# Linear attention and MLP on one core: first tiles in another order, key weights by halves, masks in parts, a query at tile 14, the last tile by halves

## The chip, the cores and the metric

The kernel runs on one core of one Trainium2 chip. The metric is the device time of one execution in microseconds. It was run three times before the change: 780.79, 780.26 and 780.09 us, median 780.26. One more execution was profiled.

## The reference

Four layers over a residual stream x of 2048 tokens by 576 channels in bfloat16: attention (A), MLP (B), A, B with the same weights. Cut to what matters:

```python
def _A_ref(x, wqkv, wo):                       # H = 32 heads of Dh = 18
    qkv = (x @ wqkv) ... q, k, v = qkv[0], qkv[1], qkv[2]
    phi = lambda t: jnp.where(t > 0, t + 1, jnp.exp(t)) + 1e-6
    pq, pk = phi(q), phi(k)
    kv = jnp.einsum("bhsd,bhse->bhde", pk, v)
    z = jnp.einsum("bhsd->bhd", pk)
    num = jnp.einsum("bhqd,bhde->bhqe", pq, kv)
    den = jnp.einsum("bhqd,bhd->bhq", pq, z)[..., None] + 1e-6
    return (num / den) ... @ wo
def _B_ref(x, w1, b1, w2, b2):                 # F = 4608
    y = _layernorm(x, axis=-1)
    h = _gelu(jnp.einsum("bsd,df->bsf", y, w1) + b1)
    return jnp.einsum("bsf,fd->bsd", h, w2) + b2

x = A_x
x = x + _A_ref(_layernorm(x, axis=-1), A_wqkv, A_wo)
x = x + _B_ref(_layernorm(x, axis=-1), B_w1, B_b1, B_w2, B_b2)
x = x + _A_ref(_layernorm(x, axis=-1), A_wqkv, A_wo)
x = x + _B_ref(_layernorm(x, axis=-1), B_w1, B_b1, B_w2, B_b2)
```

## The kernel before

**Tiles.** x stays in SBUF as 16 tiles of 128 tokens (`x_sb`). A normalized tile y is transposed into `yT`, five blocks of 128 channels by 2048 tokens, of which the last block is half zeros. All weights are loaded once and stay.

**Order.** Each engine executes its instructions in the order in which the program writes them down: the helper class at L44 ties every instruction of VectorE (DVE), ScalarE (ACT), GpSimd (POOL) and SyncE (SP) to the one before it, so that nearly all of them carry the line L52 in the profile, and `pe` (L159) does the same for TensorE, whose matmuls carry L166. Waits between engines are put in from what each instruction reads and writes. So a step that is written earlier runs earlier on every engine that it uses, and an engine that waits holds up all that is written behind.

**Loads.** `load_x(t)` brings a tile of x (one DMA of 144 KB), `load_wkv(a, b)` columns a to b of the key and value weights (two DMAs: 512 rows, and 64 rows). SP issues x 0, x 1, all key columns (0 to 576), x 2, the first 252 value columns, x 3, the other value columns, x 4 to 9, then the query weights (seven DMAs), x 10 to 15, and in the tile loop the weights for later, one piece a tile.

**Head.** `warm` issues matmuls on zeros (L236: 12 of them, and 4 more at L753 behind the first transposes). `Norm` (L256) makes one normalized tile in steps that the program places one by one: `half_stats` and `close_stats` (two `bn_stats`, one `bn_aggr` and a small sum for the variance plus epsilon, all on DVE), `rstd` (a power on POOL, and on ACT's tiles a second product there), `norm` (y on DVE or ACT), `transposed` (five transposes on TensorE and a copy by ACT or DVE, or a DVE transpose and DMAs).

**Attention, tile loop** (`layer_A`, L386). For a tile t: `k_proj` makes keys in two halves of 288 columns, each with five matmuls into a PSUM bank and one exp by ACT; its `finish` on DVE makes phi with one operation on both halves and one on each half. `v_proj` makes values in two groups of columns (252 and 324) in one pair of banks, `accB`, of which there is a single one; ACT copies 504 of the columns out and DVE the last 72. `kv_acc` adds pk times v over all tiles in the pair `accA`. In the first layer (`placed` false) keys are made one tile ahead and the norms run two to three tiles ahead in the same loop; in the third layer (`placed` true) the rows were normalized in the MLP before.

**Queries.** There are 20 query blocks (5 groups of heads by 4 chunks of 512 tokens), each of five matmuls of 512 columns, an exp and a relu on ACT and two sums on DVE. `q_next` takes the next of them. With `late`, the two sums are put off and done by `finish(n)`. Before, tiles 3 to 10 (first layer) or 4 to 11 (third) issue one each, one stands behind the loop, two behind the last `kv_acc`, and the others in the code that follows.

**Behind the loop.** The last `kv_acc` releases the mask product `kvT` on DVE (it reads `maskz`), and this the sums `z_ps`, the products with wo, the denominators (`den_stage`) and the output (`wo_stage`), interleaved with query blocks and with the norms of the first four MLP tiles.

**Masks.** `masks_a` and `masks_b` build six constant tiles on POOL by fills and `affine_select`. They are called behind tiles 12 and 13 of the first layer.

**Last tile.** In the MLP (`LayerB.run`) one tile's output is 36 x 2 matmuls that alternate between the two halves of 288 columns, then `residual` adds x and bias in one DVE operation, and in the last layer the tile goes out with one DMA.

Of the kernel before, what the change touches and what calls it, by code (L numbers as in the profile page):

```python
# [15 lines left out]
P = 128  # L16
# [4 lines left out]
G = 5  # L21
# [14 lines left out]
def build(tc, A_x, A_wqkv, A_wo, B_w1, B_b1, B_w2, B_b2, out, n_layers=4):  # L36
    nc = tc.nc
    with ExitStack() as ctx:
# [60 lines left out]
        def masks_a():  # L99
            sel, fill = pool.affine_select, pool.memset  # L100
            fill(maskz[:], 1.0)
            sel(out=maskz[:], in_=maskz[:], compare_op=ALU.is_ge, fill=0.0,
                base=0, pattern=[[-DH, 7], [0, DH]], channel_multiplier=1)
            sel(out=maskz[:], in_=maskz[:], compare_op=ALU.is_ge, fill=0.0,
                base=DH - 1, pattern=[[DH, 7], [0, DH]], channel_multiplier=-1)
            sel(out=maskz[:], in_=maskz[:], compare_op=ALU.not_equal, fill=1.0,
                base=-126, pattern=[[0, 7], [0, DH]], channel_multiplier=1)
            fill(z_row[:], 0.0)
            sel(out=z_row[:], in_=z_row[:], compare_op=ALU.not_equal, fill=1.0,
                base=-126, pattern=[[0, 1]], channel_multiplier=1)  # L110
            fill(head_sel[:], 1.0)
            sel(out=head_sel[:], in_=head_sel[:], compare_op=ALU.is_ge, fill=0.0,
                base=0, pattern=[[126, G], [-DH, H]], channel_multiplier=1)
            sel(out=head_sel[:], in_=head_sel[:], compare_op=ALU.is_ge, fill=0.0,
                base=DH - 1, pattern=[[-126, G], [DH, H]], channel_multiplier=-1)

            fill(zsel[:], 0.0)
            sel(out=zsel[:, 0, :], in_=zsel[:, 0, :], compare_op=ALU.not_equal, fill=1e-6,
                base=-126, pattern=[[0, H]], channel_multiplier=1)

        def masks_b():
            sel, fill = pool.affine_select, pool.memset
            fill(quad_mask[:], 1.0)
            sel(out=quad_mask[:], in_=quad_mask[:], compare_op=ALU.is_ge, fill=0.0,
                base=0, pattern=[[-32, 4], [0, P]], channel_multiplier=1)
            sel(out=quad_mask[:], in_=quad_mask[:], compare_op=ALU.is_ge, fill=0.0,
                base=31, pattern=[[32, 4], [0, P]], channel_multiplier=-1)
            fill(head_bc[:], 0.0)
            hb = head_bc[:, :, 0:126].rearrange("p g (h d) -> p g h d", h=7)
            for quad in range(4):  # L130
                sel(out=hb, in_=hb, compare_op=ALU.not_equal, fill=1.0,
                    base=-32 * quad, pattern=[[-7, G], [-1, 7], [0, DH]], channel_multiplier=1)
# [89 lines left out]
        load_wkv(0, D)  # L222
# [13 lines left out]
        warm(NWARM + 2)  # L236
# [19 lines left out]
        class Norm:  # L256
# [13 lines left out]
            def close_stats(self):  # L270
                stt = self.stt
                self.mv = work.tile([P, 2], F32, name="ln_mv", bufs=8)
                vec.bn_aggr(out=self.mv[:], in_=stt[:])
                self.u = work.tile([P, 1], F32, name="ln_u", bufs=8)
                if self.kind == "A":
                    vec.tensor_scalar(out=self.u[:], in0=self.mv[:, 1:2], scalar1=EPS, scalar2=None, op0=ALU.add)
                else:
                    vec.tensor_scalar(out=self.u[:], in0=self.mv[:, 1:2], scalar1=1.0 + EPS, scalar2=EPS * EPS,
                                            op0=ALU.mult, op1=ALU.add)

            def rstd(self):
# [104 lines left out]
        def layer_A(li, next_kind, before_tile, mid_tile, rows_ahead, after_tile, q_tiles, placed, mlp):  # L386
# [76 lines left out]
            if ahead:  # L463
                k_proj(0)
# [387 lines left out]
```

## Time and profile before

| What | Value |
|---|---|
| Median of three executions | 780.26 us |
| The profiled execution | 780.55 us |
| Its span, first to last instruction | 778.8 us |
| Granted TensorE clock, mean | 1.000 |
| TensorE matmul busy | 768.2 us (99%), 6563 instructions |
| VectorE busy | 285.5 us (37%) |
| ScalarE busy | 315.9 us (41%) |
| GpSimd busy | 96.3 us (12%), 174 instructions |
| DMA | 25.69 MB, in the first 58 us near all of the 16 engines' time |

In a timeline line the columns are: start in us from the beginning of the span, busy us, engine, line, operation, output and inputs by the program's names, shapes, and how many instructions were merged; in brackets the idle time of the engine before it and what ended that. PE is TensorE's matmul, PEld its weight load, SPq a DMA that SP issues. The end of a matmul is modelled, so the next may begin before the end that is shown.

### The profile page before, as it was taken

Reading aid. Unit: us, or ns where it says so; the run is one execution under the profiler, and the core shown is the slowest. Engines: PE = TensorE matmul, PEld = TensorE weight load, DVE = VectorE, ACT = ScalarE, POOL = GpSimd, SP = SyncE. Lnnn points to the kernel's source line nnn. Section 1 sums busy time; section 2 is a strip of 40 time slices with the busy share of each in tenths; the row PEclk is TensorE's granted clock in tenths of the full one; section 3 lists DMA queues with packets and bytes.
Section 4 is the critical chain, followed back from the end, with each engine's and each line's share of the span. In section 5 each row is a group of like instructions: output and inputs, shape, how many; then the busy total and the mean of one; then the engine's idle time right before and its main releaser. Section 6 shows DMA issues by size and latency. Waiting matters only on the chain.

```text
span 778.8 us, 15414 instructions
## 1 busy us (share of the span) xinstructions
PE 768.2 (99%) x6563; PEld 489.2 (63%) x6583; DVE 285.5 (37%) x700; ACT 315.9 (41%) x656; POOL 96.3 (12%) x174
## 2 busy tenths in 40 slices
PE   8999999999999999999999999999999999999998
PEld 5775555675477457646777754557745764675476
DVE  7885853436223412500354576534140230110000
ACT  4667744203720660174035577341066027305700
POOL 3114200212011101200200010002120120010010
PEclk9999999999999999999999999999999999999999
DMA  8990000010001101010000000000100100010000
GB/s 217 251 343 6 1 1 2 1 35 18 19 3 32 36 1 28 8 35 1 2 11 24 1 2 1 1 2 17 42 10 1 40 26 2 8 50 10 1 8 24
DMA packets 50334, 25.69 MB, mean 33 GB/s; under 512 B 35098, under 2 KB 50266, under 8 KB 50266
## 3 DMA queue, kind: packets, MB, share of 16 engines
q1 hardware_dynamic: 50266, 24.71, 11.6%
q8 instruction: 51, 0.84, 0.5%
q14 instruction: 17, 0.14, 0.1%
HBM read 15.79 MB, written 2.36 MB: 23 GB/s over the span
## 4 chain that ended last, share of the span: by engine, by line
PE 91%; ACT 4%; DVE 3%; issue 1%; POOL 0%; DVEq 0%; POOLq 0%
PE m_ps L166 36%; PE h_ps L166 19%; PE hp_ps L166 15%; PE v_ps L166 5%; PE k_ps L166 5%; PE q_ps L166 4%; ACT units L52 3%; PE wo_ps L166 3%; PE kvacc L166 1%; PE warm_ps L166 1%; DVE x_sb L52 1%; PE rden_ps L166 1%; DVE units L52 1%; PE tp L314 1%; DVE ln_st L52 1%
## 5 line engine op out<-in xcount | busy, mean ns | idle before, releaser
L166 PEld LDWEIGHTS <-units 128*128 128x128 bf16 (+2 forms) x2624 | 254.5, 98 | 75.8 <-issue 10.9
L166 PE MATMUL m_ps<-w_sb,units 128*128 128x288 bf16 x2304 | 283.6, 286 | 0.0
L166 PEld LDWEIGHTS <-w_sb 64*128 64x128 bf16 x2304 | 124.5, 94 | 138.1 <-issue 7.7
L166 PE MATMUL hp_ps<-yT,w_sb 64*128 64x512 bf16 x1152 | 175.7, 376 | 0.0
L166 PE MATMUL h_ps<-yT,w_sb 64*128 64x512 bf16 x1152 | 151.2, 376 | 1.0 <-DVE units L52 0.6
L52 ACT COPY relay_sb<-relay_sb 128x1 f32<-128x1 f32 x144 | 27.5, 191 | 289.4 <-PE h_ps L166 268.0
L52 DVE TENSOR_TENSOR x_sb<-m_ps,xo 128x576 bf16<-128x576 f32 x32 | 24.2, 757 | 323.4 <-PE m_ps L166 323.4
L52 ACT ACTIVATE units<-h_ps,b1T 128x512 bf16<-128x512 f32 x144 | 91.2, 684 | 44.5 <-PE h_ps L166 42.6
L52 ACT ACTIVATE units<-hp_ps,b1T 128x512 bf16<-128x512 f32 x144 | 96.2, 688 | 0.0
L52 POOL TENSOR_TENSOR xo<-x_sb,b_bc 128x576 f32<-128x576 bf16 x32 | 40.8, 1274 | 420.1 <-DVE x_sb L52 249.1
L166 PEld LDWEIGHTS <-yT 128*128 128x128 bf16 x640 | 61.0, 97 | 19.0 <-issue 1.9
L52 POOL TENSOR_TENSOR ln_rstd<-ln_u,neg_half 128x1 f32<-128x1 f32 x64 | 35.1, 549 | 209.2 <-DVE ln_u L52 209.2
L166 PE MATMUL h_ps<-yT,w_tail 64*128 64x512 bf16 x144 | 54.1, 376 | 0.0
L166 PE MATMUL hp_ps<-yT,w_tail 64*128 64x512 bf16 x144 | 54.1, 376 | 0.0
L52 DVE BATCH_NORM_STATS2 ln_st<-x_sb 128x6 f32<-128x288 bf16 x128 | 51.5, 442 | 2.3 <-DMA x_sb<-in_A_x_dram 1.9
L52 ACT ACTIVATE units<-q_ps 128x512 bf16<-128x512 f32 x80 | 43.4, 603 | 14.5 <-PE q_ps L166 9.9
L52 DVE STREAM_TRANSPOSE shared<-y_ring 128x640 bf16<-128x640 bf16 x40 | 33.3, 837 | 42.6 <-DMA yT<-shared 40.7
L166 PE MATMUL q_ps<-yT,wq_sb 128*128 128x512 bf16 x186 | 47.1, 379 | 1.2 <-ACT units L52 0.3
L166 PE MATMUL wo_ps<-shared,units 126*128 126x288 bf16 (+1 forms) x320 | 44.9, 286 | 1.0
L166 PE MATMUL v_ps<-wkv_sb,yT 128*128 128x252 bf16 (+1 forms) x320 | 44.4, 285 | 1.4 <-DVE v_ring L52 1.4
L166 PE MATMUL k_ps<-wkv_sb,yT 128*128 128x288 bf16 x320 | 44.3, 286 | 0.0
L52 DVE TENSOR_TENSOR x_sb<-wo_ps,x_sb 128x576 bf16<-128x576 f32 x32 | 24.2, 757 | 50.8 <-PE wo_ps L166 49.6
(69 smaller groups left out, 393.9 us busy)
## 6 DMA issues: line engine op xcount, KB each, us to landing
yT<-shared SPq DMA_DIRECT2D x160, 40.0 KB, 1.9
w_sb<-in_B_w_dram SPq DMA_DIRECT2D x12, 432.0 KB, 8.2
w_sb<-in_B_w_dram SPq DMA_DIRECT2D x9, 512.0 KB, 8.7
x_sb<-in_A_x_dram SPq DMA_DIRECT2D x16, 144.0 KB, 3.4
out_dram<-x_sb SPq DMA_DIRECT2D x16, 144.0 KB, 1.7
wkv_sb<-in_A_wqkv_dram SPq DMA_DIRECT2D x1, 576.0 KB
w_tail<-in_B_w_dram SPq DMA_DIRECT2D x2, 288.0 KB, 11.5
wo_sb<-in_A_wo_dram SPq DMA_DIRECT2D x1, 567.0 KB
```

Source lines behind the costliest of these rows:

```text
L52: inst = issue(*args, **kw)
L166: return pe(nc.tensor.matmul(out_, lhsT=lhsT, rhs=rhs, start=start, stop=stop, **kw))
L314: pe(nc.tensor.transpose(out=tp[:, k, :], in_=self.y[:, k * P:(k + 1) * P], identity=ident[:]))
```

## The change

1. **Key weights by halves.** The 576 key columns come with two calls of `load_wkv` instead of one, that is four DMAs instead of two.
2. **First tiles.** The warm-up is 9 matmuls, not 12. The zeroing of the query weights' padding on POOL (five fills) comes ahead of the first norm. Behind the first tile's transposes, `begin0` writes out the order: key halves, transposes of tiles 1 and 2, statistics of tiles 2 and 3, phi, and the values of tile 0 in two parts. In tile 0 of the loop phi of tile 1 stands around the norm of tile 3.
3. **Variance sum.** It goes from DVE (`close_stats`) to POOL (`rstd`), for all 64 norms.
4. **Masks in parts.** Nine batches, one behind each of the tiles 2 to 10 of the first layer; the first instruction of a batch waits for the DVE's copy of that tile's values.
5. **Query at tile 14.** Tile 14 of both attention layers issues a query; one of the two behind the last `kv_acc` is gone, and one `finish` less stands later.
6. **Values of tile 0 in the third layer.** ACT copies all 576 columns.
7. **Last tile by halves.** In the last layer tile 15 makes its 36 matmuls of the first half, adds and stores it, then the second half.

```diff
-        load_wkv(0, D)
+        load_wkv(0, HALF)
+        load_wkv(HALF, D)
...
-        warm(NWARM + 2)
+        warm(NWARM - 1)
...
                 vec.bn_aggr(out=self.mv[:], in_=stt[:])
-                self.u = work.tile([P, 1], F32, name="ln_u", bufs=8)
...
+            def rstd(self):
+                u = work.tile([P, 1], F32, name="ln_u", bufs=8)
                 if self.kind == "A":
-                    vec.tensor_scalar(out=self.u[:], in0=self.mv[:, 1:2], scalar1=EPS, scalar2=None, op0=ALU.add)
+                    pool.tensor_scalar(out=u[:], in0=self.mv[:, 1:2], scalar1=EPS, scalar2=None, op0=ALU.add)
...
-                pool.tensor_tensor(out=self.r[:], in0=self.u[:], in1=neg_half[:], op=ALU.pow)
+                pool.tensor_tensor(out=self.r[:], in0=u[:], in1=neg_half[:], op=ALU.pow)
...
-        def masks_a():
...
-        def masks_b():
...
+        def mask_batches():
...
+            def quads_b():
+                first = sel(out=quad_mask[:], in_=quad_mask[:], compare_op=ALU.is_ge, fill=0.0,
+                            base=31, pattern=[[32, 4], [0, P]], channel_multiplier=-1)
+                fill(head_bc[:], 0.0)
+                return first
...
+            return [maskz_a, maskz_b, heads, quads_a, quads_b] + [spread(quad) for quad in range(4)]
...
+            def v_copy(t, whole=False):
+                va, vp = v_ring[state["vcnt"] % NV], vps.pop(t)
                 state["vcnt"] += 1
...
                 vas[t] = va
+                if whole:
+                    act.copy(out=va[:, 4, 0:72], in_=vp[:, 1, 252:324])
+                    return lambda: None
                 return lambda: vec.tensor_copy(out=va[:, 4, 0:72], in_=vp[:, 1, 252:324])
...
+            if not placed:
+                begin(k_half, k_exp, k_sum, v_half)
             for t in range(NT):
                 before_tile(t)
-                if t + ahead < NT:
-                    k_proj(t + ahead)
-                if not ahead or t == 0:
-                    k_finish[t]()
+                if placed:
+                    k_proj(t)
+                    k_finish(t)
+                elif 0 < t < NT - 1:
+                    k_proj(t + 1)
                 mid_tile(t)
                 finish(len(q_late))
-                if 1 <= t < NT - 1 and ahead:
+                if 1 <= t < NT - 1 and not placed:
                     kv_acc(t - 1)
-                v_finish = v_proj(t)
-                if ahead and t + 1 < NT:
-                    k_finish[t + 1]()
-                rows_ahead(t)
-                v_finish()
-                if t >= 1 and (t == NT - 1 or not ahead):
+                if t == 0 and not placed:
+                    v_last = v_copy(t)
+                else:
+                    v_last = v_proj(t, placed and t == 0)
+                if not placed and t == 0:
+                    k_exp(1)
+                    k_sum(1, 0)
+                    rows_ahead(0)
+                    k_sum(1, 1)
+                elif not placed and t + 1 < NT:
+                    k_finish(t + 1)
+                    rows_ahead(t)
+                done = v_last()
+                if t >= 1 and (t == NT - 1 or placed):
                     kv_acc(t - 1)
                 if t in q_tiles:
                     q_next(True)
-                after_tile(t)
+                after_tile(t, done)
...
             finish(1)
-            q_next(True)
             q_next(True)
             zp = one("z_ps")
...
-            finish(5)
+            finish(4)
...
                         acc = pair("m2_ps")
+                        if t == NT - 1 and li == n_layers - 1:
+                            for half in range(2):
+                                cols = slice(half * HALF, (half + 1) * HALF)
+                                for f in range(NF):
+                                    mm(acc[:, half, 0:HALF], hT[f][:, j * P:(j + 1) * P], w2_sb[:, f, cols],
+                                       f == 0, f == NF - 1)
+                                vec.tensor_tensor(out=x_sb[:, t, cols], in0=acc[:, half, 0:HALF],
+                                                  in1=xo_of[t][:, cols], op=ALU.add)
+                                sp.dma_start(out=out_f[t * P:(t + 1) * P, cols], in_=x_sb[:, t, cols])
+                            break
...
+        zero_pads()
         norms[0].stats()
         norms[0].rstd()
...
         norms[1].norm()
-        norms[1].transposed()
-        norms[2].stats()
-        norms[2].rstd()
-        zero_pads()
         load_wq()
...
+        def begin0(k_half, k_exp, k_sum, v_half):
+            k_half(0, 0)
+            norms[1].transposed()
+            k_half(0, 1)
+            k_half(1, 0)
+            norms[2].stats()
+            norms[2].rstd()
+            k_half(1, 1)
+            k_exp(0)
+            k_sum(0, 0)
+            norms[2].norm()
+            k_sum(0, 1)
+            v_half(0, 0, range(3))
+            norms[2].transposed()
+            norms[3].stats()
+            norms[3].rstd()
+            v_half(0, 0, range(3, KD))
+            v_half(0, 1)
...
         def mid_tile0(t):
             if t == 0:
-                norms[2].norm()
+                return
...
-            if t == NT - 4:
-                masks_a()
-            if t == NT - 3:
-                masks_b()
+            if 2 <= t < 2 + len(batches):
+                first = batches[t - 2]()
+                tc.add_manual_dep(first.ins, done.ins.name, SYNC, reason="beside VectorE's statistics")
...
-                layer_A(li, nk, before_tile0, mid_tile0, rows_ahead0, after_tile0, range(3, 11), False, mlps.get(li + 1))
+                layer_A(li, nk, begin0, before_tile0, mid_tile0, rows_ahead0, after_tile0, (*range(3, 11), NT - 2), False,
+                        mlps.get(li + 1))
             elif kind == "A":
-                layer_A(li, nk, lambda t: lnq.tick(), nothing, nothing, nothing, range(4, 12), True, mlps.get(li + 1))
+                layer_A(li, nk, None, lambda t: lnq.tick(), nothing, nothing, lambda *a: None, (*range(4, 12), NT - 2), True,
+                        mlps.get(li + 1))
```

`k_half`, `k_exp`, `k_sum` and `v_half` are the former bodies of `k_proj`, its `finish` and `v_proj`, cut at the halves; the instructions are the same.

## The prediction

> **What bounds the kernel now.** I read the page's busy table and chain first, then the first 16 us, the end of the first layer's tile loop, the start and end of the second such loop, and the end of the span, each as a timeline.
>
> ```profile
> PE 768.2 (99%) x6563; PEld 489.2 (63%) x6583; DVE 285.5 (37%) x700; ACT 315.9 (41%) x656; POOL 96.3 (12%) x174
> PE 91%; ACT 4%; DVE 3%; issue 1%; POOL 0%; DVEq 0%; POOLq 0%
> ```
>
> TensorE is busy for 768.2 of 778.8 us and makes 91% of the chain. No transfer or other engine can give much: what is left is 10.6 us in which TensorE stands, and matmuls that only fill time. So I ask of each edit which TensorE gap it closes. The head first:
>
> ```profile
> 1.31 5.30 PE L166 MATMUL warm_ps<-y_ring 128*128 128x512 bf16 x12 [1.31 <-DVE y_ring L52]
> ...
> 4.08 0.15 DVE L52 TENSOR_SCALAR ln_u<-ln_mv 128x1 f32<-128x1 f32 x1
> ...
> 4.32 0.56 POOL L52 TENSOR_TENSOR ln_rstd<-ln_u,neg_half 128x1 f32<-128x1 f32 x1 [1.87 <-DVE ln_u L52]
> ...
> 6.40 0.57 PE L314 MATMUL tp<-ident,y_ring 128*128 128x128 bf16 x5
> ...
> 7.96 2.61 PE L166 MATMUL k_ps<-wkv_sb,yT 128*128 128x288 bf16 x20
> 8.26 0.82 DVE L52 BATCH_NORM_STATS2 ln_st<-x_sb 128x6 f32<-128x288 bf16 x2 [1.03 <-DMA x_sb<-in_A_x_dram]
> ...
> 11.60 0.45 PE L314 MATMUL tp<-ident,y_ring 128*128 128x128 bf16 x5 [1.03 <-DVE y_ring L52]
> ...
> 14.61 0.42 PE L166 MATMUL kvacc<-pk,v_ring 128*128 128x126 bf16 x5
> ```
>
> Twelve warm-up matmuls hold TensorE until 6.40, though the first normalized tile is ready at 4.91 + 0.43 = 5.34. The first key matmul starts at 7.96; the small piece of the key weights, issued at 2.17, landed 5.8 us later (7.97). Tile 2 of x landed at 8.26, and its statistics and norm make TensorE wait until 11.60. From there TensorE runs without a gap. Now the end of the tile loop:
>
> ```profile
> 62.09 1.39 PE L166 MATMUL v_ps<-wkv_sb,yT 128*128 128x252 bf16 x10
> 62.47 1.02 DVE L52 TENSOR_SCALAR phi_e<-phi_e 128x576 bf16<-128x576 bf16 x1 [0.77 <-ACT phi_e L52]
> 62.70 0.63 POOL L52 MEMSET head_bc<- 128x640 bf16 x1
> ...
> 63.57 0.58 ACT L52 CAST v_ring<-v_ps 128x504 bf16<-128x504 f32 x1 [1.13 <-PE v_ps L166]
> ...
> 64.61 1.39 PE L166 MATMUL v_ps<-wkv_sb,yT 128*128 128x252 bf16 x10 [1.13 <-DVE v_ring L52]
> ```
>
> Tile 15's v needs the one v buffer back: TensorE stands from 62.09 + 1.23 = 63.32 to 64.61. The second layer has a smaller case (k of tile 1 ends at 398.28):
>
> ```profile
> 398.45 0.22 DVE L52 CAST v_ring<-v_ps 128x72 bf16<-128x72 f32 x1
> ...
> 398.72 1.39 PE L166 MATMUL v_ps<-wkv_sb,yT 128*128 128x252 bf16 x10 [0.27 <-DVE v_ring L52]
> ```
>
> And the end, where a whole tile's sum and its store follow the last matmul:
>
> ```profile
> 775.48 0.76 DVE L52 TENSOR_TENSOR x_sb<-m_ps,xo 128x576 bf16<-128x576 f32 x1 [8.06 <-PE m_ps L166]
> 776.27 0.33 SPq L52 DMA_DIRECT2D out_dram<-x_sb  x1
> ```
>
> **The change, part by part.**
>
> *Head: 0.3 us gained.* The variance sum moves from DVE to POOL. From the end of the aggregate (4.05) to the power took 0.27 us; on POOL it is 0.07 to start, 0.265 for a 128x1 tensor-scalar (the ln_nmr group's mean) and 0.10 to the power (86.40 to 86.50 in such a pair): 0.44. So y of tile 0 is ready at 5.51. Nine warm-ups of 0.427 end at 5.15, the transposes start at 5.56 instead of 6.40, yT follows 1.30 later (7.70 less 6.40) at 6.86, and the four warm-ups in between end near 7.25. Key matmuls of tile 0, first half, start there; five of 0.122 take 0.61, tile 1's transposes 0.28, so the second half comes at 8.14, or when its weights land. SP issues two more DMAs (some 1.0 us by the x2 row at 1.69), ahead of tile 2 and the v weights, but tile 2 lands 5.5 us after its issue, queued behind key weights, so the issue is covered. Behind them SP waited until 7.64 for a weight to land before it issued tile 4, which lands 3.4 later, at 11.0, and is first read at 14.16: 3 us of cover. Packets: in 4 to 5 us 285 packets took 99% of 16 engines (56 ns for 1.1 KB), in 6 to 7 us 513 took 114% (36 ns for 0.62 KB). Halving 576 rows of 1152 B adds 576 x (2 x 34 - 56) / 16 = 0.4 us by that, nothing if bytes alone count, 2.0 if every packet costs 56 ns. I take 0.35, near the small packets' row: tile 2 at 8.61.
>
> Then DVE sets the pace. On ACT exp 0.41 and the yT copy 0.69 come before the second exp, which ends at 9.56. DVE: statistics and aggregate of tile 2 to 9.67, then phi; half of pk; y of tile 2 when POOL is done (9.67 + 0.44 + 0.55 + 0.04 = 10.70); half of pk at 11.04; statistics of tile 3 at 11.4 to 12.45; phi; half of pk; y of tile 3 at 13.48; half of pk at 13.8; the v copy of tile 0 at 14.16 to 14.40. So kvacc starts at 14.45 instead of 14.61. With tile 2 at 8.26 the same list starts from the exp and ends at 14.05: gain 0.5. I take 0.3. TensorE could have come to this point 1.03 us earlier (v of tile 0 ends at 12.08, not 13.11), which is the upper end; with the 2.0 us packets the list ends near 16.1, a loss of 1.5, which is the lower. The pad memsets on POOL (1.14 us at 10.23) move to 2.45, where POOL has nothing until 4.3; if that cover were gone they would delay the first power by up to 1.1.
>
> *Masks on POOL: nothing.* Some 10 us of fills and selects leave 57.5 to 67.5 for nine batches of 1.0 to 1.3 us, each waiting for the DVE's v copy of tiles 2 to 10. Behind it in POOL's queue is only the next tile's rstd; it may come 0.3 us late, while y of a tile with a query is written at 30.30 and first read at 32.52. That 1.8 us is the cover.
>
> *Query to tile 14, first layer: 1.15 us.* Five 216 ns matmuls (1.08) fill the 1.29 gap. Without the head_bc fill beside it, phi takes its 0.31, the v copy follows ACT's (64.15 + 0.04), ends at 64.42, and v of tile 15 starts at 64.46 instead of 64.61: 0.15. One of the two queries behind the last kvacc goes: the mask product (67.93, 0.82 long) then runs with one query beside it and z_ps starts 0.06 after both, near 68.81 less the 0.15. Before it was 69.81. So 1.15 in all.
>
> *Query to tile 14, second layer: 0.25 us lost.* Its tile 14 has no gap, so 1.08 is put in and taken out. But the query's sums now stand on DVE before tile 15's v copy. After the query of tile 11 that copy ended at 439.96, 4.02 after the tile's first key matmul; kvacc of tile 15 wants it after 1.23 + 1.23 + 0.27 + 1.08 = 3.81. It waits 0.25 with the semaphore. Bounds 0 and 0.5.
>
> *v of tile 0 copied whole by ACT, second layer: 0.44 us.* ACT is free at 397.84; 72 columns cost about 0.25, so the buffer is free at 398.13, before k ends at 398.28. v starts there and not at 398.72. Its next exp loses 0.25, which waits for TensorE until 398.49 anyway.
>
> *Last tile by halves: 0.36 us.* The sum on 288 columns is 0.42 (the 128x288 rows) for 0.76; the store of half the bytes perhaps 0.02 less. 72 matmuls and 72 weight loads stay; the store more, 0.33 on SP, is issued 4.4 us before the end.
>
> *POOL's longer rstd between the layers: nothing.* DVE loses a 0.15 us step from its chain at 82.33, the third norm gains 0.17 on POOL at 85.85. Bounds -0.2 and 0.2 for each layer.
>
> Sum: 0.3 + 1.15 - 0.25 + 0.44 + 0.36 = 2.0. The profiled run took 780.55 us (span 778.8, 1.75 around it), 0.29 above the median of 780.26. 780.55 - 2.0 - 0.29 = 778.3.
>
> **The rivals.** *The head gains all:* if DVE's list is shorter than I add it up, the head gives 1.0: 777.6. For it: DVE runs such a list elsewhere with overlaps of 0.1. Against: the waits for POOL are real in it.
>
> *The clock comes later.* Warm-up matmuls are 0.427 apart up to 6.40, and the four at 6.81 took 1.03, the last ones 0.22 apart: full speed came in just there. The new head issues three fewer and leaves TensorE idle for 0.4 us near 5.3. If full speed then comes 3.4 us later, key matmuls cost 0.24: the second exp of tile 0 ends at 10.9 instead of 9.6, the list shifts by 1.25, and the time is 779.5. For it: only the long series is seen to precede the change. Against: only 0.4 us are open.
> The Trainium skill, TensorE: Matmul & The Clock Gate, Part 1, says that the clock is released after a busy window of about 3.4 us, and Part 4 that transposes don't count as busy; by that rule the time is this rival's if the window sees too little. The trace agrees with the doubling, and doesn't show the threshold.
>
> *Slower: mask batches block DVE.* The phi at 62.47 took 1.02 instead of 0.31, beside a fill. If every such operation waits for POOL, then after each of nine v copies DVE does statistics (1.09) and waits until POOL has done batch, sum and power (2.1): 1.0. A tile with a query has 4.07 us for some 3.5 of DVE work, so 0.45 is lost nine times, 4.0: 782.3. It outweighs the gain of 2.0 when the wait passes 0.57 + 2.0 / 9 = 0.79. Against: the y at 57.95 and the phi at 59.48 ran beside selects in their usual 0.42 and 0.31. The batches end 0.1 to 0.3 after the statistics.
> The Trainium skill, GPSIMD Engine Reference, 1. Specifications, lists the SBUF interfaces as shared with VectorE, with contention in its two-port modes. By that rule selects would hold DVE too; the rows at 57.95 and 59.48 speak against it, that at 62.47 for it.
>
> *The last tile's halves don't overlap:* if the second half's matmuls wait for the first half's sum, 0.06 + 0.42 + 0.05 = 0.53 is added: 778.8. Nothing in the trace shows a case; the two halves lie in separate banks.
>
> **How the numbers follow.** A measurement here tells about 0.2%, 1.56 us, from no change, so faster means under 778.7, slower over 781.8. Chances: forecast 0.52 (its own range 777.6 to 779.0), head gains all 0.14, late clock 0.18, blocked DVE 0.10, no overlap at the end 0.06. Faster: 0.44 + 0.14 + 0.02 + 0.02 = 0.62. Slower: the blocked DVE, 0.10. The rest, 0.28, is the same. The range 777.0 to 779.9 leaves out the blocked DVE, the worst packets and little else.
>
> **What would show it.** First transposes near 5.6 and first key matmul near 7.25; kvacc of tile 0 at 14.1 to 14.5; tile 14's query before a v at some 64.3; z_ps some 1.15 us after the last kvacc's end instead of 2.2; no gap before v of tile 1 in the second layer; a last sum of 0.42. Wrong: 0.24 us key matmuls (clock), phi or query sums over 0.5 in tiles 3 to 11 (POOL), tile 2 later than 8.9 (packets).

## The result and the profile after

| | before | after |
|---|---|---|
| Median (lowest to highest), nine runs each | 780.21 us (780.02 to 780.79) | 777.96 us (777.90 to 778.32) |
| The profiled execution, its span | 780.55, 778.8 us | 777.94, 776.2 us |

The ratio is 0.9971 with a 95% interval of 0.9960 to 0.9981: 2.25 us faster, where 1.96 was forecast (780.26 less 778.3).

From the page of the changed kernel, the busy time of each engine and the chain of waits by engine:

```profile
PE 767.1 (99%) x6559; PEld 488.2 (63%) x6580; DVE 274.3 (35%) x636; ACT 315.8 (41%) x657; POOL 113.1 (15%) x238
PE 91%; ACT 4%; DVE 3%; issue 1%; POOL 0%; DMA 0%; DVEq 0%; POOLq 0%
```

TensorE still makes 91% of the chain. DVE lost 11.2 us of busy time and POOL gained 16.8, and the shares of the chain stay as they were: what counts is which of TensorE's gaps a step ends. The head, as a timeline of the changed kernel (matmuls now carry L181, transposes L330):

```profile
1.31 3.61 PE L181 MATMUL warm_ps<-y_ring 128*128 128x512 bf16 x9 [1.31 <-DVE y_ring L52]
...
4.16 0.23 POOL L52 TENSOR_SCALAR ln_u<-ln_mv 128x1 f32<-128x1 f32 x1 [0.49 <-DVE ln_mv L52]
...
5.57 0.45 PE L330 MATMUL tp<-ident,y_ring 128*128 128x128 bf16 x5 [0.65 <-DVE y_ring L52]
...
6.81 0.79 PE L181 MATMUL k_ps<-wkv_sb,yT 128*128 128x288 bf16 x5
...
7.47 0.81 DVE L52 BATCH_NORM_STATS2 ln_st<-x_sb 128x6 f32<-128x288 bf16 x2
...
8.85 1.40 PE L181 MATMUL k_ps<-wkv_sb,yT 128*128 128x288 bf16 x10 [0.17 <-ACT yT L52]
...
9.16 0.31 DVE L52 TENSOR_SCALAR phi_e<-phi_e 128x576 bf16<-128x576 bf16 x1 [0.63 <-ACT phi_e L52]
...
9.88 0.42 DVE L52 TENSOR_SCALAR y_ring<-x_sb,ln_mv,ln_rstd 128x576 bf16<-128x576 bf16 x1
...
13.12 0.45 PE L330 MATMUL tp<-ident,y_ring 128*128 128x128 bf16 x5
...
13.35 0.22 DVE L52 CAST v_ring<-v_ps 128x72 bf16<-128x72 f32 x1
...
13.41 0.42 PE L181 MATMUL kvacc<-pk,v_ring 128*128 128x126 bf16 x5
```

TensorE is free at 4.92 and waits 0.65 for the first y. The first keys start at 6.81, and the statistics of tile 2 name no DMA any more. The first phi waits for the second exp on ACT (0.63). kvacc of tile 0 comes at 13.41, earlier than the 14.1 to 14.5 that was forecast. The end of the first layer's tile loop, and v of tile 1 in the third layer:

```profile
60.89 1.39 PE L181 MATMUL v_ps<-wkv_sb,yT 128*128 128x252 bf16 x10
61.27 0.31 DVE L52 TENSOR_SCALAR phi_e<-phi_e 128x576 bf16<-128x576 bf16 x1 [0.77 <-ACT phi_e L52]
...
62.33 1.03 PE L181 MATMUL q_ps<-yT,wq_sb 128*128 128x512 bf16 x4
...
63.27 1.39 PE L181 MATMUL v_ps<-wkv_sb,yT 128*128 128x252 bf16 x10
...
394.69 0.70 ACT L52 CAST v_ring<-v_ps 128x504 bf16<-128x504 f32 x2 [0.81 <-PE v_ps L181]
...
395.72 1.39 PE L181 MATMUL v_ps<-wkv_sb,yT 128*128 128x252 bf16 x10
```

The query stands where the gap of 1.29 was (four of its five matmuls are recorded), phi takes 0.31 instead of 1.02, and in the third layer v starts without a wait. The end of the span:

```profile
763.53 0.76 DVE L52 TENSOR_TENSOR x_sb<-m_ps,xo 128x576 bf16<-128x576 f32 x1 [8.06 <-PE m_ps L181]
...
767.94 0.46 DVE L52 TENSOR_TENSOR x_sb<-m_ps,xo 128x288 bf16<-128x288 f32 x1 [3.65 <-PE m_ps L181]
768.45 4.57 PE L181 MATMUL m_ps<-w_sb,units 128*128 128x288 bf16 x36 [0.62 <-DVE x_sb L52]
...
773.06 0.46 DVE L52 TENSOR_TENSOR x_sb<-m_ps,xo 128x288 bf16<-128x288 f32 x1 [4.66 <-PE m_ps L181]
```

The last sum is short, but the second half's matmuls stood 0.62 for the first half's sum: the rival that was given 0.06 is what happened.

Where each kernel stands at the same points of TensorE's work (start of the first matmul named, us). "Before, again" is a second profile of the kernel before, told of below; the gain is counted against it:

```
                     before  before, again  after   gain so far  gain of the step
kvacc, tile 0         14.61      14.13      13.41      0.72          0.72
z_ps, first layer     69.81      69.34      67.39      1.95          1.23
first h_ps            90.79      90.31      88.23      2.08          0.13
k, third layer       394.61     394.11     392.04      2.07         -0.01
kvacc, third layer   399.95     399.44     396.94      2.50          0.43
z_ps, third layer    450.41     449.90     447.42      2.48         -0.02
first h_ps, fourth   471.39     470.87     468.27      2.60          0.12
last sum starts      775.48     774.94     773.06      1.88         -0.72
last sum ends        776.24     775.70     773.52      2.18          0.30
```

Behind the first kvacc these stretches can be read closely: in profiles that share the code of a stretch, its length agrees within 0.04 us, whatever went on in the head. For instance, the stretch from kvacc of tile 0 to z_ps takes 53.98 us in the changed kernel and in all experiments on it but the two that alter this stretch.

### The profile page after: what moved, and what is told of

The parts are those of the page before. It is cut to its first block, busy times and chain, and to the rows that moved or that the text cites. A ratio compares the mean times of both kernels' runs of the same rounds, so it can differ in the third digit from the quotient of the medians.

```text
span 776.2 us, 15424 instructions
## 1 busy us (share of the span) xinstructions
PE 767.1 (99%) x6559; PEld 488.2 (63%) x6580; DVE 274.3 (35%) x636; ACT 315.8 (41%) x657; POOL 113.1 (15%) x238
## 4 chain that ended last, share of the span: by engine, by line
PE 91%; ACT 4%; DVE 3%; issue 1%; POOL 0%; DMA 0%; DVEq 0%; POOLq 0%
PE m_ps L181 36%; PE h_ps L181 19%; PE hp_ps L181 15%; PE v_ps L181 5%; PE k_ps L181 5%; PE q_ps L181 4%; ACT units L52 3%; PE wo_ps L181 3%; PE kvacc L181 1%; DVE units L52 1%; PE rden_ps L181 1%; DVE x_sb L52 1%; DVE ln_st L52 1%; PE tp L330 1%; PE kvwo_ps L181 0%
## 5 line engine op out<-in xcount | busy, mean ns | idle before, releaser
L181 PEld LDWEIGHTS <-units 128*128 128x128 bf16 (+2 forms) x2624 | 254.5, 98 | 76.6 <-issue 11.7
L181 PE MATMUL m_ps<-w_sb,units 128*128 128x288 bf16 x2304 | 283.8, 286 | 0.6 <-DVE x_sb L52 0.6
L181 PEld LDWEIGHTS <-w_sb 64*128 64x128 bf16 x2304 | 124.6, 94 | 138.1 <-issue 7.7
L181 PE MATMUL hp_ps<-yT,w_sb 64*128 64x512 bf16 x1152 | 175.7, 376 | 0.0
L181 PE MATMUL h_ps<-yT,w_sb 64*128 64x512 bf16 x1152 | 151.1, 376 | 1.0 <-DVE units L52 0.6
L52 DVE TENSOR_TENSOR x_sb<-m_ps,xo 128x576 bf16<-128x576 f32 (+1 forms) x33 | 24.4, 739 | 323.1 <-PE m_ps L181 323.1
L181 PEld LDWEIGHTS <-yT 128*128 128x128 bf16 x640 | 60.8, 97 | 18.7 <-ACT yT L52 1.1
L181 PE MATMUL h_ps<-yT,w_tail 64*128 64x512 bf16 x144 | 54.1, 376 | 0.0
L181 PE MATMUL hp_ps<-yT,w_tail 64*128 64x512 bf16 x144 | 54.1, 376 | 0.0
L181 PE MATMUL q_ps<-yT,wq_sb 128*128 128x512 bf16 x185 | 47.4, 379 | 0.8
L181 PE MATMUL wo_ps<-shared,units 126*128 126x288 bf16 (+1 forms) x320 | 44.9, 286 | 1.0
L181 PE MATMUL k_ps<-wkv_sb,yT 128*128 128x288 bf16 x320 | 44.6, 286 | 0.2 <-ACT yT L52 0.2
L181 PE MATMUL v_ps<-wkv_sb,yT 128*128 128x252 bf16 (+1 forms) x320 | 44.6, 285 | 0.0
L52 DVE TENSOR_SCALAR y_ring<-x_sb,ln_mv,ln_rstd 128x576 bf16<-128x576 bf16 x58 | 30.7, 529 | 28.2 <-POOL ln_rstd L52 28.2
```

Source lines behind the costliest of these rows:

```text
L52: inst = issue(*args, **kw)
L181: return pe(nc.tensor.matmul(out_, lhsT=lhsT, rhs=rhs, start=start, stop=stop, **kw))
```

## The experiments

Each takes the changed kernel and edits one thing, unless it says otherwise. Times are medians; each is compared with the changed kernel's 777.96. The experiments ran on three chips, on which the kernel before took 780.07, 780.14 and 780.28 (780.21 beside the changed kernel), so a difference of 0.1 to 0.2 between two medians tells nothing by itself; where it matters, the stretches of the traces are given.

**The last tile, each half in a bank and a tile of its own.**

```diff
-                        acc = pair("m2_ps")
                         if t == NT - 1 and li == n_layers - 1:
                             for half in range(2):
+                                acc = one("m2_half")
```

> The changed kernel with the two halves of the last tile in two PSUM tiles of one bank each, instead of the two banks of one pair tile. Theory: in the changed kernel's trace the second half's matmuls begin 0.51 us after the first half's sum has begun and 0.62 us of idle TensorE stand before them, because the two halves share one tile and the program's waits are set by the tile; with two tiles the gap is gone and the time falls by 0.6, from 777.96 to 777.35. Rival: TensorE and VectorE can't use the two banks at once for a reason that lies in the chip; then the gap and the time stay.

Measured: 777.36 us (777.23 to 777.67), ratio to the kernel before 0.9964 (0.9952 to 0.9977): 0.60 faster. Its timeline at the end, where m_ps is the tile before:

```profile
763.70 8.98 PE L181 MATMUL m_half<-w_sb,units 128*128 128x288 bf16 x72
763.97 0.76 DVE L52 TENSOR_TENSOR x_sb<-m_ps,xo 128x576 bf16<-128x576 f32 x1 [8.06 <-PE m_ps L181]
...
768.38 0.46 DVE L52 TENSOR_TENSOR x_sb<-m_half,xo 128x288 bf16<-128x288 f32 x1 [3.65 <-PE m_half L181]
...
772.72 0.46 DVE L52 TENSOR_TENSOR x_sb<-m_half,xo 128x288 bf16<-128x288 f32 x1 [3.88 <-PE m_half L181]
```

All 72 matmuls run as one series beside the first half's sum, and the 0.62 is gone. The halves lay in two banks in both versions, so the wait was made by their being one tile of the program, not by the banks. From the start of the sum of tile 14 to the end of the last sum it takes 9.21 us here and 9.99 in the changed kernel.

**The last tile whole again.**

```diff
-                        if t == NT - 1 and li == n_layers - 1:
+                        if False:
```

> The changed kernel with the last tile made and added as a whole, as before the change. Theory: the halves cost 0.62 of waiting and give 0.30 by the shorter last sum (0.46 for 0.76) and a little by the shorter store, so without them the time falls by 0.2 to 0.3, to 777.7. The recorded prediction, in which the halves overlap, says that it rises by 0.36, to 778.3.

Measured: 777.59 us (777.47 to 778.03), ratio 0.9968 (0.9956 to 0.9980). Undoing this part makes the kernel 0.37 faster: as written, it cost what it was forecast to gain. The stretch named above takes 9.58 us, 0.41 less than in the changed kernel and 0.37 more than with a tile for each half.

**Key weights in one piece again.**

```diff
-        load_wkv(0, HALF)
-        load_wkv(HALF, D)
+        load_wkv(0, D)
```

> The changed kernel with all key columns in one load (two DMAs instead of four). Theory 1: the halves matter little, since the first half landed at 5.2 and is first used at 6.8, and whole keys land by 6.9 where no DMA engine lags: the first key matmuls come 0.1 to 0.2 later, tile 2 of x lands 0.35 earlier, time 777.8 to 778.1. Theory 2: the halves are what the head gained beyond the prediction; whole keys land near 8.0, as in the profile of the kernel before, and the time rises by 0.8 to 1.1, to about 778.9.

Measured: 777.82 us (777.70 to 778.12), ratio 0.9971 (0.9959 to 0.9982): no difference that the medians tell. Tile 2 lands at 7.10 here and at 7.28 in the changed kernel (up to 7.70 in the other profiles with halves). But the second profile of the kernel before, with whole keys too, has 7.70, so the landings don't show what the packets cost. DVE is ready for tile 2 only at 7.46, and the keys of a whole load are there by 6.79, so neither the packets nor the earlier first half reaches TensorE. The trace is 0.16 shorter than the changed kernel's behind the last sum (2.55 us to the end of the span, where it is 2.71).

**Twelve warm-up matmuls again.**

```diff
-        warm(NWARM - 1)
+        warm(NWARM + 2)
```

> The changed kernel with 12 warm-up matmuls instead of 9. Theory 1: the head's pace is set by the chain first transposes, yT, keys, exp, phi; 12 warm-ups hold the first transposes from 5.57 to 6.4 when the clock comes late and to some 5.9 when it comes at 4.4, so the time rises by 0.3 to 0.8, to 778.3 to 778.7. Theory 2: tile 2 of x and VectorE's list behind it set the pace (as the prediction has it); then it rises by no more than 0.2. If the fewer warm-ups delayed the clock (the rival of the prediction), 12 would be faster than 9, by up to 1.2.

Measured: 778.50 us (777.90 to 778.68), ratio 0.9977 (0.9968 to 0.9986): 0.54 slower in the median, but three of the ten executions took 777.90 to 777.96, no longer than the changed kernel. The profiled one took 778.66. In its timeline:

```profile
6.40 0.61 PE L330 MATMUL tp<-ident,y_ring 128*128 128x128 bf16 x5
...
7.72 0.82 DVE L52 BATCH_NORM_STATS2 ln_st<-x_sb 128x6 f32<-128x288 bf16 x2
...
7.80 0.79 PE L181 MATMUL k_ps<-wkv_sb,yT 128*128 128x288 bf16 x5
...
9.96 0.31 DVE L52 TENSOR_SCALAR phi_e<-phi_e 128x576 bf16<-128x576 bf16 x1 [1.18 <-ACT phi_e L52]
```

The transposes come 0.83 later and the first keys 0.99; kvacc of tile 0 follows at 14.21, 0.80 later. Part of that is the clock, which came to full speed at 6.7 here and at 4.4 in the changed kernel's profile: with nine warm-ups and full clock at 6.9 kvacc stood at 13.75, so by these two profiles the three warm-ups make 0.46 where the clock is late. That the three short executions are those with an early clock was not shown. DVE stands idle for 1.18 until the second exp is there, with tile 2's statistics long done. So the chain of transposes, yT, keys and exp sets the pace here, not tile 2's landing.

**The old order behind the first transposes** (keys behind tile 1's transposes and tile 2's statistics, both parts of pk ahead of the next norm, the values of tile 0 in one part).

```diff
+            norms[1].transposed()
+            norms[2].stats()
+            norms[2].rstd()
             k_half(0, 0)
-            norms[1].transposed()
             k_half(0, 1)
...
             k_sum(0, 0)
-            norms[2].norm()
             k_sum(0, 1)
+            norms[2].norm()
```

> The changed kernel with the instructions of the first tiles in the order that they had before (transposes of tile 1 and statistics of tile 2 ahead of all keys, phi of tile 0 in one piece ahead of the norm of tile 2, values whole, phi of tile 1 whole ahead of the norm of tile 3); 9 warm-ups and key halves stay. Theory: the order gives what the fewer warm-ups don't: the first keys wait for tile 1's transposes (0.3 to 0.9 later), y of tile 2 and of tile 3 come behind all of pk (0.4 each), and the time rises by 0.4 to 0.8, to 778.4 to 778.8. Rival: the warm-ups alone did it, which gave 0.54 back when they were put in again; the order is worth less than 0.15.

Measured: 778.89 us (778.70 to 778.96), ratio 0.9982 (0.9973 to 0.9991): 0.93 slower, a little more than expected. From its timeline:

```profile
7.66 0.45 PE L330 MATMUL tp<-ident,y_ring 128*128 128x128 bf16 x5 [0.72 <-DVE y_ring L52]
...
7.95 2.61 PE L181 MATMUL k_ps<-wkv_sb,yT 128*128 128x288 bf16 x20
...
10.90 0.42 DVE L52 TENSOR_SCALAR y_ring<-x_sb,ln_mv,ln_rstd 128x576 bf16<-128x576 bf16 x1
```

The first keys wait behind tile 1's transposes, and these for y (0.72). y of tile 2 comes at 10.90 instead of 9.88: 0.66 of that is phi, which waits for a later exp (9.82 for 9.16), and the rest is the second part of pk, now written ahead of it. Full clock came at 4.3 here, as early as in the changed kernel's profile, and kvacc of tile 0 at 14.40: the order is worth 0.99 there.

**The kernel before, profiled a second time**, on the chip that the old order ran on.

> The kernel before, unchanged, profiled a second time. Theory: in the first profile one of the DMA engines lagged by 1.2 us at tile 2 of x (15 of 16 had landed by 7.03, the last at 8.24); here tile 2 lands near 7.1 as in the profile with whole keys, and the first keys still start near 7.96, since the warm-ups and tile 1's transposes hold them. Rival: the lag belongs to this kernel, and tile 2 lands after 8 again.

Measured: 780.02 us, one execution, span 778.3. From its timeline:

```profile
7.34 0.45 PE L314 MATMUL tp<-ident,y_ring 128*128 128x128 bf16 x5 [0.39 <-DVE y_ring L52]
...
7.63 2.61 PE L166 MATMUL k_ps<-wkv_sb,yT 128*128 128x288 bf16 x20
7.72 0.82 DVE L52 BATCH_NORM_STATS2 ln_st<-x_sb 128x6 f32<-128x288 bf16 x2 [0.44 <-DMA x_sb<-in_A_x_dram]
...
9.50 0.31 DVE L52 TENSOR_SCALAR phi_e<-phi_e 128x576 bf16<-128x576 bf16 x1 [0.53 <-ACT phi_e L52]
...
10.58 0.48 DVE L52 TENSOR_SCALAR y_ring<-x_sb,ln_mv,ln_rstd 128x576 bf16<-128x576 bf16 x1
...
14.13 0.42 PE L166 MATMUL kvacc<-pk,v_ring 128*128 128x126 bf16 x5
```

Tile 2 landed at 7.70, neither at the 7.1 that was expected nor at 8.24. In the first profile 15 of its 16 DMA engines were done by 7.03 and one came 1.2 us later, as it did for the key weights ahead of it. That delay belonged to one execution. The first profile has at the same place:

```profile
9.82 0.31 DVE L52 TENSOR_SCALAR phi_e<-phi_e 128x576 bf16<-128x576 bf16 x1 [0.31 <-ACT phi_e L52]
...
10.91 0.63 DVE L52 TENSOR_SCALAR y_ring<-x_sb,ln_mv,ln_rstd 128x576 bf16<-128x576 bf16 x1
```

In both, DVE is done with tile 2's statistics and then stands for the second exp (0.31 and 0.53), so not even the landing at 8.24 held DVE's list. Up to kvacc of tile 0 the two profiles differ by 0.48. 0.32 of it is there by phi (9.82 and 9.50), behind warm-ups that end later, since full clock came at 6.7 in the first profile and at 4.9 in the second. The other 0.15 is y of tile 2, which took 0.63 us for 0.48; POOL's fills of the query weights' padding ran beside it in both, and in the changed kernel, where they come earlier, the same y took 0.42.

**No query at tile 14 of the first layer** (the second one behind the last kvacc is back).

```diff
-                (*range(3, 11), NT - 2), False,
+                range(3, 11), False,
...
+            if not placed:
+                q_next(True)
```

> The changed kernel without the query at tile 14 of the first layer; two queries stand behind the last kvacc there, as before the change. Theory (the recorded step): TensorE stands for about 1.1 us before v of tile 15 and z_ps comes 1.08 later after the last kvacc, so the time rises by 1.0 to 1.15, to 779.0 to 779.1. Rival: a query behind the last kvacc covers the mask product as well as it fills the gap, so the place doesn't matter: 778.0.

Measured: 779.05 us (778.94 to 779.44), ratio 0.9985 (0.9977 to 0.9994): 1.09 slower. The timeline has the old gap again, 0.99 as the trace counts it:

```profile
60.87 1.39 PE L181 MATMUL v_ps<-wkv_sb,yT 128*128 128x252 bf16 x10
...
63.25 1.39 PE L181 MATMUL v_ps<-wkv_sb,yT 128*128 128x252 bf16 x10 [0.99 <-DVE v_ring L52]
```

v of tile 15 starts at the same time with the query (63.27) and without it (63.25): the query was free.

**No query at tile 14 of the third layer.** The same edit for `placed`.

> The changed kernel without the query at tile 14 of the third layer; two queries stand behind the last kvacc there. Theory: no change, 777.9 to 778.05, since the changed kernel's trace has the last kvacc start as soon as its query is done, while the last v copy is still running (446.07 against 446.02), and z_ps comes 2.99 earlier than before where v of tile 13 comes 3.00 earlier. The recorded step, in which the kvacc waits 0.25 for that copy, says 777.7.

Measured: 777.91 us (777.84 to 778.06), ratio 0.9971 (0.9960 to 0.9983): no difference. In the changed kernel, where the query's sums stand ahead of v's copy:

```profile
445.68 0.43 DVE L52 TENSOR_TENSOR units<-units 128x512 bf16<-128x512 bf16 x1
...
446.02 0.23 DVE L52 CAST v_ring<-v_ps 128x72 bf16<-128x72 f32 x1
446.07 0.44 PE L181 MATMUL kvacc<-pk,v_ring 128*128 128x126 bf16 x5
```

The copy is as late as forecast, up to 446.25, but kvacc starts at 446.07: its first four matmuls read the 504 columns of ACT, and only the fifth reads these 72.

**Masks behind tiles 12 and 13 again.**

```diff
-            if 2 <= t < 2 + len(batches):
-                first = batches[t - 2]()
...
+            if t == NT - 4:
+                for batch in batches[:3]:
+                    batch()
+            if t == NT - 3:
+                for batch in batches[3:]:
+                    batch()
```

> The changed kernel with the masks built behind tiles 12 and 13 as before the change, without the waits for the v copies. Theory (the recorded step): the batches are hidden at tiles 2 to 10, and late masks only lengthen phi of tile 15 by 0.7, of which 0.15 is not covered by the query: 778.1. Rival: the batches cost VectorE and GpSimd time beside each other in nine tiles (in the changed kernel's trace a query's first sum takes 0.37 on average against 0.28 before, the power 0.77 against 0.55), and without them the time falls by 0.3 or more, to 777.6.

Measured: 777.96 us (777.88 to 778.41), ratio 0.9972 (0.9962 to 0.9983), equal to the changed kernel's. The masks' place is worth nothing, either way. The 0.15 that was expected for phi beside the fill did not come either: that phi took 0.48 here, where it was 1.02 before the change, and the query covers it.

**The variance sum on DVE again.**

```diff
                 vec.bn_aggr(out=self.mv[:], in_=stt[:])
+                u = self.u = work.tile([P, 1], F32, name="ln_u", bufs=8)
...
-                    pool.tensor_scalar(
+                    vec.tensor_scalar(
```

> The changed kernel with the variance sum on VectorE again for all 64 norms. Theory (the recorded steps): y of tile 0 comes 0.17 earlier, VectorE's list in the head and in the two chains between the layers is 0.1 to 0.15 longer at each norm; together the time stays within 0.2 of 777.96. Rival: the sum on GpSimd is what shortens the head beyond the prediction (TensorE's wait for tile 3 there), and the time rises by 0.4 or more.

Measured: 778.40 us (778.23 to 778.96), ratio 0.9978 (0.9969 to 0.9987): 0.44 slower, the size that the rival gave but not at its place. The head is 0.34 faster with the sum on DVE (kvacc of tile 0 at 13.07). It is lost again: 0.10 up to z_ps, 0.13 before the first h_ps of each MLP, and 0.37 at tile 13 of the third layer:

```profile
435.58 0.82 DVE L52 SCALAR_TENSOR_TENSOR pk<-k_ps,phi_e 128x288 bf16<-128x288 f32 x2 [0.47 <-PE v_ps L181]
...
437.26 1.39 PE L181 MATMUL v_ps<-wkv_sb,yT 128*128 128x252 bf16 x10 [0.34 <-DVE v_ring L52]
```

There pk waits until TensorE's values matmuls of that stretch are done, and the v copy behind it on DVE comes late. In the changed kernel the same pk starts right behind phi:

```profile
434.92 0.31 DVE L52 TENSOR_SCALAR phi_e<-phi_e 128x576 bf16<-128x576 bf16 x1 [1.75 <-ACT phi_e L52]
...
435.33 0.82 DVE L52 SCALAR_TENSOR_TENSOR pk<-k_ps,phi_e 128x288 bf16<-128x288 f32 x2
```

No norm runs at that place; why pk waits there was not tried.

**v of tile 0 in the third layer copied by DVE again.**

```diff
-                    v_last = v_proj(t, placed and t == 0)
+                    v_last = v_proj(t)
```

> The changed kernel with the last 72 columns of tile 0's values in the third layer copied by VectorE, as before. Theory (the recorded step): v of tile 1 waits for that copy behind VectorE's two pk sums, 0.43, and the time rises by that, to 778.4. Rival: VectorE has less to do since the variance sum left it, and the wait shrinks to 0.3 or less.

Measured: 778.20 us (778.15 to 778.43), ratio 0.9974 (0.9964 to 0.9984): 0.24 slower. In its timeline the copy ends at 396.18 and v starts at 396.24, 1.43 after the keys of tile 1; with ACT's copy it is 1.22, and before it was 1.66. So of the 0.43 that this place gave, 0.2 is ACT's copy. The other 0.23 is there with the copy still on DVE, as the expectation's rival has it: the 0.15 sum is no longer in DVE's list ahead of the copy, and phi starts 0.12 after the keys where it was 0.31.

**The best of it**: banks of their own for the last halves, key weights in one piece, and two warm-ups instead of four behind the first transposes.

```diff
-        warm(4)
+        warm(2)
```

> The changed kernel with three edits that the runs so far point to: the last tile's halves in two PSUM tiles, key columns in one load, and two instead of four warm-ups behind the first transposes. Theory: the first edit gives 0.6; whole keys cost nothing; with a clock that comes at 6.2 to 7.0, four warm-ups end at 7.1 to 7.4, after yT is ready at 6.8, and two of them end before, so the first keys gain 0.2 to 0.4 more: 776.9 to 777.3. Rival: with two fewer the clock comes a window of 3.4 us later, key matmuls take 0.24, and the time rises to 778 or more.

Measured: 777.02 us (776.96 to 777.14), ratio 0.9959 (0.9945 to 0.9973). It beats both kernels: 0.94 under the changed one. The profiled executions, 777.94 and 777.02, tell where. kvacc of tile 0 stands at 13.41 in the changed kernel and at 13.43 here, and the stretches from there to the last tiles are alike, so the two edits in the head gave nothing up to there in these two executions, both with an early clock. The stretch of the last tile is 0.78 shorter (9.21 for 9.99), and from the last sum to the end of the span it is some 0.15 shorter (2.57 for 2.71), as with key weights in one piece alone (2.55). Why whole keys shorten the end was not tried.

## Why the prediction held, and where it did not

The sign, the size and the largest term were right. That the sum came out was luck: against the second profile of before, the head gave 0.42 more than forecast, the third layer's query 0.23 and the stretches before the two MLPs together 0.25, while the last tile gave 0.78 less. Of the rivals, "the head gains all" came in good part and "the halves don't overlap" in full, with opposite signs.

- **Query at tile 14, first layer: right.** 1.15 was forecast. The step up to z_ps gave 1.23, and taking it back cost 1.09. The gap took the query without delay, and phi without the fill beside it gave 0.14 for the 0.15 forecast.
- **Head: right in sign, too small.** 0.3 was forecast; 0.72 is measured against the second profile of before, 1.20 against the first. The step that failed is "Then DVE sets the pace", which started DVE's list from tile 2's landing at 8.61. Already in the first profile the list did not start from the landing (8.26 there): phi waited 0.31 for the second exp, so the landing was not what made TensorE wait until 11.60, as the prediction reads that trace. Now tile 2 lands at 7.28 and waits for DVE.

  kvacc of tile 0 was put at 14.45 and came at 13.41. By the prediction's own working 0.40 of this is the landing (its list ends at 14.05 where it starts from the exp). 0.43 is the second exp, which ended at 9.13 and not at 9.56. The rest, 0.2, is kvacc itself, which the prediction put behind the v copy: it starts beside it (13.41 and 13.35). The length of the list, 4.2 from the end of the second exp to the v copy, was right.

  The exp came early because the first keys came at 6.81 and not at 7.25: full clock came at 4.4 us and not at 6.7, and the four warm-ups ended sooner. In the two profiles with the same head in which it came at 6.9 and 7.0, the first keys came at 7.35 and 7.43 and kvacc at 13.75 and 13.84.

  By single profiles the order gives 0.99 and the sum's move takes 0.34 back, which leaves 0.65 of the 0.72; the fewer warm-ups count only where full clock comes late. The packet term of 0.35 is not shown by the landings (7.10 to 7.70 with whole keys where no engine was late, 7.28 to 7.70 with halves), and it is hidden behind DVE in any case.
- **Late clock: did not happen.** Key matmuls kept their length (five in 0.79, ten in 1.40). The rule of the Trainium skill, TensorE: Matmul & The Clock Gate, Part 1, that the window runs freely and doesn't start with the kernel, agrees with the traces: full clock came at 4.4 us after nine warm-ups, at 6.7 with twelve, and at 6.7 and 4.9 in two profiles of the kernel before. The window's length, which the prediction found in no trace, shows in the fourteen traces together: the stretch at full clock lasted 768.0, 771.4 or 774.8 us, in steps of 3.41.
- **Variance sum: right in the head, wrong behind it.** That it delays the first y was right: the first y starts 0.13 later than in the second profile of before, and the head without this move is 0.34 faster. "Nothing" between the layers was too low, though within its bounds: with the sum on DVE the kernel loses 0.13 before each MLP. For the 0.37 at tile 13 of the third layer the prediction had no term, and its cause stays open. Together the move is worth 0.44 net of the head.
- **Query at tile 14, third layer: wrong.** -0.25 was forecast, 0 measured. The step "kvacc of tile 15 wants it" took the whole kvacc to need the 72 columns; its fifth matmul alone does.
- **v of tile 0 in the third layer: right in sum, not in cause.** 0.44 was forecast and 0.43 came, but ACT's copy alone is 0.20 to 0.24.
- **Last tile by halves: wrong in sign.** +0.36 was forecast; 0.37 is gained by taking it back. The step that failed is the reason "the two halves lie in separate banks". They do, but both belong to one `pair` tile, and the wait is set by tile: the rival's mechanism, with 0.62 of idle time where it had worked out 0.53. With a tile for each half the forecast's mechanism holds, and its size: the stretch of the last tile falls from 9.58 to 9.21, 0.37 for the 0.36 forecast. The medians, 777.59 and 777.36, differ by 0.23.
- **Masks: right.** Nothing was forecast and nothing came, though a sign that was named for the rival is there: sums over 0.5 beside a select. From the changed kernel's timeline:

```profile
30.77 0.64 POOL L52 TENSOR_SCALAR_AFFINE_SELECT quad_mask<-quad_mask 128x512 bf16<-128x512 bf16 x1
...
31.00 0.56 DVE L52 TENSOR_SCALAR units<-units 128x512 bf16<-128x512 bf16 x1
```

In the groups by form from 17 to 62 us, the same sum over all eight tiles with a query, in the changed kernel:

```profile
L52 DVE TENSOR_SCALAR units<-units 128x512 bf16<-128x512 bf16 x8 | 3.0, 372 | 0.0
```

The same group with the masks late again:

```profile
L52 DVE TENSOR_SCALAR units<-units 128x512 bf16<-128x512 bf16 x8 | 1.9, 240 | 0.0
```

The mean is 372 ns beside the masks and 240 with the masks late: 0.13 for each of eight tiles, far under the 0.57 of cover that the rival had to use up. The Trainium skill, GPSIMD Engine Reference, 1. Specifications, which lists the SBUF interfaces as shared with VectorE, is borne out by these rows in kind; here it decides nothing.

## What to carry to other kernels

When TensorE is busy for 99%, list its few gaps and ask of each edit which one it closes: a query block of 1.08 us put into a gap made about half of the 2.25. To let a sum run beside the next matmuls, give the halves tiles of their own, since in this program a wait is kept by tile and not by bank. Before a forecast is built on a late landing, look whether the instruction behind it waited for something else besides, as phi did for the exp; look also whether one DMA engine alone was late in that execution, or profile the kernel twice. And compare two profiles by stretches rather than by their spans: behind the head they agree within 0.04 us where the code is the same.

## What the runs showed of the hardware that was not expected

- Full clock, by the trace's record of the clock, came at any time from 4.0 us (the best version) to 7.0 us (that with only the halves in banks of their own), behind the same nine warm-ups. From the changed kernel, at 4.4, to the one at 7.0 the first keys move from 6.81 to 7.43 and kvacc of tile 0 from 13.41 to 13.84, with no edit in the head: such a difference between two single profiles says nothing of an edit. Early or late makes no difference up to 5.8 us (kvacc at 13.39 to 13.46 in the three profiles with full clock at 4.4, 4.7 and 5.8); from 6.2 on it does (13.47 at 6.2, 13.51 and 13.55 at 6.4, 13.75 at 6.9, 13.84 at 7.0).
- One DMA engine of 16 came 1.2 us behind the others with tile 2 in one execution; in the other thirteen profiles the last came at most 0.33 behind. The statistics of tile 2 began at 8.26, behind that last engine (8.24).
- POOL's power became longer with the sum's move, not with the masks. By the groups from 17 to 62 us, in the changed kernel:

```profile
L52 POOL TENSOR_TENSOR ln_rstd<-ln_u,neg_half 128x1 f32<-128x1 f32 x11 | 8.4, 767 | 0.9
```

With the sum on DVE and the masks in the same place:

```profile
L52 POOL TENSOR_TENSOR ln_rstd<-ln_u,neg_half 128x1 f32<-128x1 f32 x11 | 6.1, 555 | 6.6 <-DVE ln_u L52 5.9
```

With the masks late it is still 801 ns. In the changed kernel the power is long (0.77 to 0.89 us) in just the eight tiles that have a query, and takes 0.57 in the others of these eleven. The sum's move shifts the power against DVE's list (at 31.72 it ran beside the query's product and phi). That this is what stretches it fits, but was not tried.
